# Mixing k with tokens on partitions, through the crossbar and GpSimd, with the mixes one unit ahead

## The chip, the cores and the metric

The kernel runs on one core of one Trainium2 chip. The metric is the device time of one execution in microseconds (us); lower is better. The kernel before took 245.54 us (median of 4 runs).

Engines are named as in the profile: PE is TensorE, PEld its weight loads, DVE is VectorE, ACT is ScalarE, POOL is GpSimd, and SP is the engine whose queue issues stores and crossbar transposes (DMA_TRANSPOSE in the trace: a transfer that also turns its data). A transfer lands when its data have arrived. The granted clock is the share of its full clock that PE was given. A run is called slow when it lies over 1.5% above the fastest run of the same kernel.

## The reference, cut to what matters

An attention over 4 batches of 8 heads (768 tokens, 64 columns a head, 8 blocks of 96 tokens) feeds a bilinear feed-forward layer. The argument turns on one line, the mixing of k's blocks, and on the scores that use it:

```python
k_sorted = np.einsum('bhij,bhjcd->bhicd', P, k_b).reshape(B, H, S, D)   # P: 8x8 a head, after 5 rounds
v_sorted = np.einsum('bhij,bhjcd->bhicd', P, v_b).reshape(B, H, S, D)
...
scores = scale * np.matmul(q_b, k_sb.transpose(0, 1, 2, 4, 3))          # per block of 96 tokens
...
return (a * b @ w_out)                                                   # a = x @ w_a, b = x @ w_b
```

## The kernel before

Heads are handled in 16 pairs, g = 0 to 15, four a batch. PE is kept busy with the feed-forward layer of one batch (`ffn_ab`, then `ffn_out`), and the attention of the next batch is woven in as twelve short units: `c_` mixes k and v of a pair, `s_` computes its scores, `o_` its output. A step of `ffn_ab` is eight matmuls of 384 columns.

```python
    def stage_mix(g, what, engines):                   # k and v alike
        ...
        for c in range(NCH):                           # NCH = 6
            for e in range(2):                         # the two heads of the pair
                nc.tensor.matmul(
                    mix[e * D:(e + 1) * D, c // 3, c % 3 * P:(c % 3 + 1) * P],
                    lhsT=src2[:, e, c * D:(c + 1) * D],
                    rhs=s_all[:, 2 * g + e], start=True, stop=True)
        # ... ACT (k) or DVE and ACT (v) copy mix into kT / vT, in block order
        if what == "v" and g > HP:                     # HP = 4
            nc.sync.dma_start_transpose(out=vss[...], in_=...)

    def units_full(b):
            def c_(g):
                if g < 2 * HP - 2:
                    turn_q(g)
                stage_mix(g, "k", ("act",))
                stage_mix(g, "v", ("dve", "act"))
                if 2 * HP - 2 <= g < B * HP - 2:
                    nc.gpsimd.tensor_copy(out=gate, in_=kTs[g % NBUF][0:1, 0:1])
                    load_pair((g + 2) // HP, (g + 2) % HP)     # POOL issues k, v, q
            def s_(g):
                stage_scores(g)                        # PE reads kT(g) and qT(g)
                # ... turn_v and stage_q for the first pairs, cut
                if 2 * HP <= g + 1 < B * HP:
                    pair_q(g + 1)                      # POOL copies q
                    stage_q(g + 1)                     # SP: crossbar transpose to qT
            ...
            for u, n in ((c_, 0), (s_, 0), (c_, 1), (s_, 1), (c_, 2), (o_, 0), (s_, 2), (c_, 3),
                         (o_, 1), (s_, 3), (o_, 2), (o_, 3)):
```

The gate is a copy of one element on POOL. It holds the next loads back until this unit's k has been mixed. In the timelines the matmuls of PE and the instructions of POOL and SP start in the order of the program (POOL below: gate at 102.53, then k, v and q at 103.04, 103.75 and 104.46).

The softmax here doesn't subtract the row's maximum and nothing guards it: scores larger than these inputs give would overflow.

## Time and profile before

| | before |
|---|---|
| median time, us | 245.54 |
| span of the profiled run, us | 243.3 |
| PE / DVE / ACT / POOL busy | 98% / 45% / 43% / 25% |
| granted clock of PE | 1.0 |
| time of the k and v mixes of a pair on PE, us | 0.79 |

First, from the page of the kernel before: busy us (share of the span) and the number of instructions, the busy tenths of PE in 40 slices, and the chain of work that ended last, by engine.

```profile
span 243.3 us, 5625 instructions
PE 237.4 (98%) x2309; PEld 141.6 (58%) x2309; DVE 109.1 (45%) x258; ACT 104.4 (43%) x204; POOL 61.4 (25%) x88
PE   7999999999999999999999999999999999999994
...
PE 93%; DVE 4%; ACT 1%; DMA 1%; issue 0%
```

PE is the limit from the first slice to the last. So any wait that the change puts in front of PE lengthens the run, and relief for ACT or DVE is worth nothing in itself.

Next, PE's timeline around the mixes of pair 10 (start us, duration us, engine, line, operation, output<-inputs, shape, count). The duration of a group includes the pipeline behind its last matmul, so groups are best compared from start to start.

```profile
99.90 0.81 PE L332 MATMUL pf<-xT,w_a_sb 128*128 128x384 bf16 x4
100.55 0.81 PE L332 MATMUL pf<-xT,w_b_sb 128*128 128x384 bf16 x4
101.30 0.53 PE L281 MATMUL mix<-s_all,k 128*64 128x128 bf16 x12
101.66 0.50 PE L281 MATMUL mix<-s_all,v 128*64 128x128 bf16 x12
102.09 0.82 PE L332 MATMUL pf<-xT,w_a_sb 128*128 128x384 bf16 x4
```

Four matmuls of 384 columns take 0.65 us (99.90 to 100.55), half a step. Twelve of 128 columns take only 0.36 us (101.30 to 101.66), 30 ns each. By proportion one of them alone would take about 54 ns (a third of 0.65/4 us; an estimate), so two of them run side by side in the halves of the array. In front of such a group PE pauses for 0.1 us (100.55 + 0.65 is 101.20).

Last, POOL's timeline behind the same mixes; the brackets give the idle time before and what ended it.

```profile
102.53 0.18 POOL L542 COPY gate<-kT 1x1 bf16<-1x1 bf16 x1 [4.45 <-ACT kT L162]
103.04 0.72 POOL L95 DMA_DIRECT2D k<-in_k_dram  x1 [0.34 <-PE pf L332]
103.75 0.72 POOL L95 DMA_DIRECT2D v<-in_v_dram  x1
104.46 0.73 POOL L95 DMA_DIRECT2D q<-in_q_dram  x1
105.18 0.85 POOL L246 COPY qc<-q 128x768 bf16<-128x768 bf16 x1
```

From the mix (101.30) to the end of the third load issue (105.18) POOL needs 3.9 us. Nothing that PE waits for stands behind it here, except q's copy, which has two units of time.

### The profile page before, as it was taken

How to read it: one execution, taken by the hardware profiler on the slowest of the kernel's cores; microseconds unless marked ns; L12 is line 12 of the kernel's file. 1: busy time of each engine (PE TensorE's matmuls, PEld its weight loads, DVE VectorE, ACT ScalarE, POOL GpSimd, SP SyncE). 2: the span in 40 equal slices, each digit the busy share in tenths (PEclk: the TensorE clock that was granted, in tenths of full speed). 3: DMA queues.
4: the chain of work that ended last, by engine and by line, in shares of the span. 5: the costliest groups of instructions: out<-in, count | busy, mean ns of one | idle time of the engine just before them, and what ended most of it. 6: DMA issues, size and time to landing. Idle time of an engine off the chain costs nothing.

```text
span 243.3 us, 5625 instructions
## 1 busy us (share of the span) xinstructions
PE 237.4 (98%) x2309; PEld 141.6 (58%) x2309; DVE 109.1 (45%) x258; ACT 104.4 (43%) x204; POOL 61.4 (25%) x88
## 2 busy tenths in 40 slices
PE   7999999999999999999999999999999999999994
PEld 7776666666554466666654466666654466665442
DVE  6774557555435234464534144363625144344110
ACT  3675853565630175736330165737330133333001
POOL 8766569623220053240400054200000000000000
PEclk9999999999999999999999999999999999999999
DMA  5999999985999589993964369923524310000132
GB/s 78 202 198 196 196 201 201 203 138 83 158 204 153 130 70 155 171 138 70 136 115 122 115 120 114 159 51 58 47 75 131 109 43 0 3 0 1 46 129 86
DMA packets 53930, 28.04 MB, mean 115 GB/s; under 512 B 30736, under 2 KB 50960, under 8 KB 53904
## 3 DMA queue, kind: packets, MB, share of 16 engines
q0 software_dynamic: 20944, 14.16, 41.6%
q1 hardware_dynamic: 32816, 13.45, 28.0%
q8 instruction: 18, 0.29, 0.5%
q14 instruction: 8, 0.07, 0.1%
q10 hardware_dynamic: 144, 0.07, 0.1%
HBM read 28.32 MB, written 6.29 MB: 142 GB/s over the span
## 4 chain that ended last, share of the span: by engine, by line
PE 93%; DVE 4%; ACT 1%; DMA 1%; issue 0%
PE pf L332 52%; PE po L377 24%; PE mix L281 4%; PE o_ps L231 3%; PE sc L302 2%; PE mixh L180 2%; PE po L362 1%; PE vs_ps L208 1%; PE xt_ps L222 1%; PE sc L195 1%; DMA p_nat<-in_sort_net_dram 1%; PE heat L168 1%; PE two L332 1%; PE q_ps L260 1%; DVE xp L237 1%
## 5 line engine op out<-in xcount | busy, mean ns | idle before, releaser
L353 DVE TENSOR_TENSOR hT<-a_sb,pf 128x384 bf16<-128x384 bf16 x95 | 52.6, 553 | 73.8 <-PE pf L332 46.4
L332 PE MATMUL pf<-xT,w_a_sb 128*128 128x384 bf16 x380 | 78.0, 326 | 0.2 <-ACT xT L162 0.2
L332 PE MATMUL pf<-xT,w_b_sb 128*128 128x384 bf16 x380 | 77.5, 326 | 0.0
L352 ACT CAST a_sb<-pf 128x384 bf16<-128x384 f32 x95 | 45.5, 479 | 60.9 <-PE pf L332 41.3
L377 PE MATMUL po<-w_out_sb,hT 128*128 128x512 bf16 x276 | 61.9, 379 | 0.0
L332 PEld LDWEIGHTS <-w_b_sb 128*128 128x128 bf16 x384 | 37.5, 98 | 24.8 <-issue 0.3
L332 PEld LDWEIGHTS <-w_a_sb 128*128 128x128 bf16 x384 | 34.9, 98 | 22.2
L377 PEld LDWEIGHTS <-hT 128*128 128x128 bf16 x276 | 26.3, 98 | 30.0
L162 ACT COPY o_sb<-po 128x512 f32<-128x512 f32 (+1 forms) x13 | 7.5, 577 | 46.8 <-PE po L377 45.2
L164 DVE COPY o_sb<-po 128x512 f32<-128x512 f32 (+1 forms) x12 | 7.9, 656 | 35.2 <-PE po L377 26.3
L307 ACT ACTIVATE eT<-sc 96x768 bf16<-96x768 f32 x24 | 18.0, 802 | 6.9 <-PE sc L302 6.9
L542 POOL COPY gate<-kT 1x1 bf16<-1x1 bf16 x8 | 1.4, 179 | 74.7 <-ACT kT L162 74.7
L237 DVE TENSOR_TENSOR xp<-o_ps,rec 96x512 bf16<-96x512 f32 x24 | 15.9, 684 | 0.6 <-DVE rec L235 0.2
L162 ACT CAST kT<-mix 128x384 bf16<-128x384 f32 x24 | 10.3, 482 | 8.0 <-PE mix L281 8.0
L95 POOL DMA_DIRECT2D k<-in_k_dram x16 | 11.6, 724 | 4.5 <-PE pf L332 2.3
L95 POOL DMA_DIRECT2D v<-in_v_dram x16 | 11.5, 721 | 3.1 <-DMA w_b_sb<-in_moe_w_b_dram 1.2
L231 PEld LDWEIGHTS <-eT 96*128 96x128 bf16 x256 | 10.4, 97 | 3.2 <-DVE xp L237 0.6
L235 DVE RECIPROCAL rec<-o_ps 96x8 f32<-96x8 f32 x32 | 5.6, 189 | 13.8 <-PE o_ps L231 13.8
L231 PE MATMUL o_ps<-vs,eT 96*128 96x65 bf16 x256 | 11.3, 193 | 0.2 <-DVE xp L237 0.2
L246 POOL COPY qc<-q 128x768 bf16<-128x768 bf16 x10 | 8.4, 842 | 7.2 <-DMA q<-in_q_dram 7.2
L95 POOL DMA_DIRECT2D q<-in_q_dram x12 | 8.7, 721 | 1.7 <-DMA w_a_sb<-in_moe_w_a_dram 0.7
L168 PE MATMUL heat<-warm 128*128 128x128 bf16 x84 | 7.6, 264 | 1.3 <-DVE warm L77 1.3
(80 smaller groups left out, 158.3 us busy)
## 6 DMA issues: line engine op xcount, KB each, us to landing
out_dram<-o_sb SPq DMA_DIRECT2D x17, 256.0 KB, 2.0
k<-in_k_dram POOLq DMA_DIRECT2D x16, 192.0 KB, 6.0
v<-in_v_dram POOLq DMA_DIRECT2D x16, 192.0 KB, 6.4
q<-in_q_dram POOLq DMA_DIRECT2D x12, 192.0 KB, 6.7
w_a_sb<-in_moe_w_a_dram POOLq DMA_DIRECT2D x6, 256.0 KB, 9.8
w_b_sb<-in_moe_w_b_dram POOLq DMA_DIRECT2D x6, 256.0 KB, 10.0
w_out_sb<-in_moe_w_out_dram POOLq DMA_DIRECT2D x3, 512.0 KB, 10.8
out_dram<-o_sb SPq DMA_DIRECT2D x12, 128.0 KB, 2.4
```

The lines of the kernel that those rows point to most:

```text
L95: nc.gpsimd.dma_start(out=to, in_=_ap(t, base, [[W, P], [S * D, 2], [1, W]]))
L162: nc.scalar.copy(out=out, in_=in_)
L168: nc.tensor.matmul(ps[:, 0:cols], lhsT=warm[:, 0:P], rhs=warm[:, 0:cols], start=True, stop=True)
L231: nc.tensor.matmul(o_ps[:, e, i * (D + 1):(i + 1) * (D + 1)], lhsT=eT[:, hf, e, i * BLK:i * BLK + P], rhs=vs[0:BLK, i0 + i, V0 - 1 + e * ( ...
L237: nc.vector.tensor_tensor(out=_ap(xp, i0 * 2 * D, [[nxp * 2 * D, BLK], [D, 2], [2 * D, NBH], [1, D]]), in0=_ap(o_ps, 1, [[1024, BLK], [511 ...
L246: nc.gpsimd.tensor_copy(out=qc.rearrange("p c e d -> p e c d"), in_=loaded[g][2].rearrange("p e (c d) -> p e c d", c=NCH))
L281: nc.tensor.matmul(mix[e * D:(e + 1) * D, c // 3, c % 3 * P:(c % 3 + 1) * P], lhsT=src2[:, e, c * D:(c + 1) * D], rhs=s_all[:, 2 * g + e], ...
L307: nc.scalar.activation(out=eT[:, hf, :, 0:HB], in_=sc[0:BLK, :, 0:HB], func=AF.Exp, scale=float(scale))
L332: nc.tensor.matmul(pf[:, 0:HW], lhsT=w_sb[:, kc, m * P:(m + 1) * P], rhs=x_cols(b, kc, t), start=(kc == 0), stop=(kc == KA - 1))
L352: nc.scalar.copy(out=a_sb, in_=pf[:, 0:HW])
L353: nc.vector.tensor_mul(out=hT[:, m, t * HW:(t + 1) * HW], in0=a_sb, in1=ab[1][:, 0:HW])
L377: nc.tensor.matmul(held["po"], lhsT=hTs[b][:, m, c * P:(c + 1) * P], rhs=w_out_sb[:, m, :], start=(m == 0), stop=(m == KO - 1))
```

## The change

The intent: k is mixed with tokens on partitions, which needs two matmuls of 384 columns in place of twelve of 128. The result has to be turned, so ACT copies it to `kn`, the crossbar transposes it to `kc`, and POOL puts it in block order into `kT`. To hide this longer path, the mixes run one unit ahead of the scores. This is done for pairs 5 to 15. In the diff, lines that only store a tile's name are left out.

```diff
+    def stage_k(g):
+        k2 = loaded[g][0]
+        mix = psA.tile([P, 2, 512], FP32, tag="A", name="mix")
+        for e in range(2):
+            nc.tensor.matmul(mix[:, e, 0:W], lhsT=s_all[:, 2 * g + e], rhs=k2[:, e],
+                             start=True, stop=True)
+        kn = att.tile([P, NCH, 2, D], BF16, tag="kn", name="kn", bufs=2)
+        copy("act", kn..., mix...)                       # (cut)
+        kc = att.tile([P, NCH, P], BF16, tag="kc", name="kc", bufs=3)
+        nc.sync.dma_start_transpose(out=kc, in_=kn.rearrange("p c e d -> p (c e d)"))
+    def order_k(g):
+        nc.gpsimd.tensor_copy(out=kTs[g % NBUF]..., in_=st[g, "kc"]...)   # (cut)
-            hTs[b] = ffp.tile([P, KO, S], BF16, tag="hT", name="hT")
+            hTs[b] = ffp.tile([P, KO, S], BF16, tag="hT", name="hT", bufs=1)
             def c_(g):
-                stage_mix(g, "k", ("act",))
+                if g > HP:
+                    stage_k(g)
+                else:
+                    stage_mix(g, "k", ("act",))
                 stage_mix(g, "v", ("dve", "act"))
                 if 2 * HP - 2 <= g < B * HP - 2:
-                    nc.gpsimd.tensor_copy(out=gate, in_=kTs[g % NBUF][0:1, 0:1])
+                    nc.gpsimd.tensor_copy(out=gate, in_=st[g, "kn"][0:1, 0, 0, 0:1])
                     load_pair((g + 2) // HP, (g + 2) % HP)
-            for u, n in ((c_, 0), (s_, 0), (c_, 1), (s_, 1), (c_, 2), (o_, 0), (s_, 2), (c_, 3),
-                         (o_, 1), (s_, 3), (o_, 2), (o_, 3)):
+            def run(u, g, then):
+                u(g)
+                if then is not None and g0 + then > HP:
+                    order_k(g0 + then)
+            for u, n, then in ((c_, 0, None), (c_, 1, 0), (s_, 0, None), (c_, 2, 1), (s_, 1, None),
+                               (o_, 0, None), (c_, 3, 2), (s_, 2, None), (o_, 1, 3), (s_, 3, None),
+                               (o_, 2, None), (o_, 3, None)):
```

More of the change, by code (lines that the diff above doesn't have):

```diff
@@ L293, in stage_mix @@
                                         in_=to.rearrange("p i t -> p (i t)"))
+    def stage_k(g):
[5 more added lines that the diff above has]
+        kn = att.tile([P, NCH, 2, D], BF16, tag="kn", name="kn", bufs=2)
+        copy("act", kn.rearrange("p c e d -> p e c d"),
+             mix[:, :, 0:W].rearrange("p e (c d) -> p e c d", c=NCH))
+        st[g, "kn"] = kn
+        kc = att.tile([P, NCH, P], BF16, tag="kc", name="kc", bufs=3)
+        nc.sync.dma_start_transpose(out=kc, in_=kn.rearrange("p c e d -> p (c e d)"))
+        st[g, "kc"] = kc
+    def order_k(g):
+        nc.gpsimd.tensor_copy(
+            out=kTs[g % NBUF][:, 0:S].rearrange("p (i c t) -> p c i t", i=NB, c=NCH),
+            in_=st[g, "kc"].rearrange("p c (i t) -> p c i t", i=NB))
     def stage_scores(g):
@@ L557, in o_ @@
                 to_xT(g)
-            for u, n in ((c_, 0), (s_, 0), (c_, 1), (s_, 1), (c_, 2), (o_, 0), (s_, 2), (c_, 3),
-                         (o_, 1), (s_, 3), (o_, 2), (o_, 3)):
-                us.append(lambda u=u, g=g0 + n: u(g))
+            def run(u, g, then):
[5 more added lines that the diff above has]
+                               (o_, 2, None), (o_, 3, None)):
+                us.append(lambda u=u, g=g0 + n, then=then: run(u, g, then))
             return us
```

## The prediction

> **What bounds it now.** The page shows TensorE busy 98% of 243.3 us, and the chain that ended last is 93% PE. From 40 us on PE runs from group to group almost without a gap, so each stall on PE that the change adds is paid in full, and work taken off ACT (43%), DVE (45%) or POOL (25%) is worth nothing in itself.
>
> **What the change saves on PE.** For 11 of 16 head pairs (g = 5 to 15) twelve k mixes of 128 columns (64 output rows each) become two of 384 columns. In the timeline of PE the twelve take 0.36 us from their start to the start of the v mixes (101.30 to 101.66): they run two at a time in the halves of the array. A group of four 384-column matmuls takes 0.65 us, 0.1625 us each. This agrees with the Trainium skill, page "TensorE: Matmul & The Clock Gate", section "Back-to-back issue gap" (columns/2.4 + 2.5 ns). So 0.36 becomes 0.325: 0.035 us a pair, 0.4 us in all (0.2%). The gap of 0.1 us before such a group stays with the v mixes.
>
> **What it moves.** ACT: two 0.48 us copies become one of 128x768, about 0.80 us (as eT and qT): nothing on the chain. SP: 11 more crossbar transposes, 1.2 us of issue, landing after 3 to 7 us like vs and qTf. POOL: 11 copies of 128x768, estimated at 0.84 us like qc. hT in one buffer costs nothing: PE reads the old one to the end first.
>
> **The new path to the scores.** kT is now written by POOL, in order, and the copy for pair g stands behind the next pair's unit: its gate, three load issues of 0.72 us, then the copy. Before, mix k to gate was 1.23 us (101.30 to 102.53), and the gate read only the first half; now it waits for the whole copy, +0.32. Gate to the end of the third issue took 2.65 us. So kT(g) is ready about 1.5 + 2.65 + 0.85 + 0.1 = 5.1 us after the next pair's mix starts. PE would reach the scores after 0.87 us and one to three steps of 1.30 us:
> - s(5), s(9), s(10): two steps, 3.47 us: stall about 1.7 us each
> - s(6): one step, 2.17 us: about 2.9 us
> - s(8), s(12): three steps, 4.77 us: about 0.4 us each
> - s(7), s(11), s(13) to s(15): no loads in front or enough steps: none, if the transposes land in 7 us.
>
> Sum about 8.8 us, less 0.4: +8.4 us, so 253.9; I say 253.5 us, range 248.5 to 258.0. Chances: faster 0.02, same 0.18, slower 0.80.
>
> **What would show it.** Wait list of PE: sc or its weight load of kT waiting for POOL's kT copy, 5 to 6 times, 0.3 to 3 us each, largest at the second scores of the first full batch (near 65 us); POOL's timeline: gate, k, v, q issue, kT copy. The kT copies show no idle wait for kc in those cases (if they do, the transposes are the late ones and the loss is larger). ACT's kn near 0.80 us; PE's clock stays at 1.0.
>
> **What would make it wrong.** If POOL's copy in runs of 16 is much slower than qc, or the load issues slow down beside more transposes (one showed 0.74 us extra at 88.9), the loss grows by 3 to 5 us. If crossbar transposes queue behind loads (qTf took up to 9.9 us to land), s(8), s(12), s(13) stall too. If PE's order gives more time than I count, it is a wash: 245.

## The result, and the profile after

| | before | after |
|---|---|---|
| median time, us | 245.54 | 257.77 (256.1 to 261.55, 4 runs) |
| span of the profiled run, us | 243.3 | 254.3 |
| PE busy | 98% | 94% |
| POOL busy | 25% | 28% |
| granted clock in the four runs | 1.0 in the profiled run | 0.993, 0.987, 0.980, 0.993 |

The ratio is 1.048 (95% interval 1.039 to 1.056): slower. Ratios are the mean time of one kernel's fast runs over that of the other's fast runs of the same rounds, so not quite the ratio of the medians. The run of 261.55 us is called slow.

From the page after, the same lines as before:

```profile
span 254.3 us, 5422 instructions
PE 238.6 (94%) x2188; PEld 140.5 (55%) x2199; DVE 109.2 (43%) x258; ACT 103.9 (41%) x193; POOL 70.0 (28%) x99
PE   8899999998599999699799999979999999999995
...
PE 81%; DMA 7%; POOL 3%; DVE 3%; issue 2%; ACT 2%; SPq 1%; ACTq 0%; POOLq 0%
```

PE's busy time rose by 1.2 us, though 110 weight loads and as many matmuls are gone (PEld: 2309 to 2199), and the row of tenths has holes. The list of PE's waits (us in total, times, longest) names two causes that the kernel before did not have:

```profile
PE sc L321 <- POOL kT L310: 5.3, 3, 2.6
PE sc L321 <- DMA qTf<-qc: 4.1, 2, 2.7
```

PE's timeline after, at the scores of pairs 5, 6, 9 and 10:

```profile
56.25 0.81 PE L351 MATMUL pf<-xT,w_b_sb 128*128 128x384 bf16 x4
58.39 0.52 PE L321 MATMUL sc<-qT,kT 64*128 64x96 bf16 x16 [1.32 <-POOL kT L310]
...
64.78 0.81 PE L351 MATMUL pf<-xT,w_b_sb 128*128 128x384 bf16 x4
68.18 0.51 PE L321 MATMUL sc<-qTf,kT 64*128 64x96 bf16 x16 [2.59 <-POOL kT L310]
...
105.05 0.81 PE L351 MATMUL pf<-xT,w_b_sb 128*128 128x384 bf16 x4
108.59 0.82 PE L321 MATMUL sc<-qTf,kT 64*128 64x96 bf16 x16 [2.73 <-DMA qTf<-qc]
109.34 1.46 PE L351 MATMUL pf<-xT,w_a_sb 128*128 128x384 bf16 x4
110.60 1.24 PE L351 MATMUL pf<-xT,w_b_sb 128*128 128x384 bf16 x4
111.67 0.81 PE L351 MATMUL pf<-xT,w_a_sb 128*128 128x384 bf16 x4
...
121.50 0.81 PE L351 MATMUL pf<-xT,w_b_sb 128*128 128x384 bf16 x4
123.67 0.51 PE L321 MATMUL sc<-qTf,kT 64*128 64x96 bf16 x16 [1.35 <-POOL kT L310]
```

Scores would start 0.65 + 0.10 us after the start of the group before them. Pair 5 started 1.39 us later than that (58.39 - 56.25 - 0.75), pair 6 2.65, pair 9 2.79. Behind pair 9's wait the next groups took 1.26 and 1.07 us in place of 0.65: PE ran at half its rate for a while, and with the scores themselves (0.75 us for 0.45) that cost 1.3 us more. The same reading gives 1.42 us for pair 10 (waiting for POOL's kT) and 1.45 us for pair 13 (167.38 - 165.18 - 0.75, waiting for q's transpose). Together: 1.39 + 2.65 + 2.79 + 1.33 + 1.42 + 1.45 = 11.0 us, which is the whole difference of the spans (254.3 - 243.3).

POOL's timeline after, at pair 10's unit, shows what stands in front of kT of pair 9:

```profile
103.71 0.18 POOL L564 COPY gate<-kn 1x1 bf16<-1x1 bf16 x1 [5.15 <-ACT kn L162]
104.16 0.72 POOL L95 DMA_DIRECT2D k<-in_k_dram  x1 [0.27 <-issue]
104.88 0.72 POOL L95 DMA_DIRECT2D v<-in_v_dram  x1
105.59 0.73 POOL L95 DMA_DIRECT2D q<-in_q_dram  x1
106.30 0.85 POOL L310 COPY kT<-kc 128x768 bf16<-128x768 bf16 x1
107.07 0.85 POOL L246 COPY qc<-q 128x768 bf16<-128x768 bf16 x1
```

The copy carries no idle time before it: `kc` had landed, and the copy only waited for its turn behind the three issues.

The late q has another origin. The next table puts together, for pair 9's neighbourhood, when each transfer was issued and when it landed (from the profile's records of issue and landing; "load(10)" is k, v and q of pair 10).

| | before: issued, landed | after: issued, landed |
|---|---|---|
| load(10), three transfers | 87.5 to 89.6, 94.2 to 96.3 | 91.3 to 93.5, 95.9 to 100.9 |
| load(11), three transfers | 95.1 to 96.5, 99.6 to 103.3 | 94.8 to 96.2, 103.0 to 106.4 |
| crossbar kc(9) | none | 94.3, 102.6 |
| crossbar vs(9) | 95.4, 101.6 | 95.6, 107.0 |
| crossbar qTf(9) | 91.2, 97.0 | 98.7, 108.5 |

In both kernels the six loads take about 15 us from the first issue to the last landing (87.5 to 103.3, and 91.3 to 106.4), which is 2.5 us a load as an estimate from these times. Before, the two gates lay 7.7 us apart (86.93 and 94.58), about what three loads need. After, two mixes follow each other with only two steps between, the gates lie 3.5 us apart (90.88 and 94.37), the six loads overlap, and q's transpose among them needs 9.8 us to land. That the distance of the gates does it is argued here; the later experiments limit this reading (see what stays open).

### The profile page after: what moved, and what is told of

It reads as the page before. It is cut to its first block, busy times and chain, and to the rows that moved or that the text cites. A ratio compares the mean times of both kernels' runs of the same rounds, so it can differ in the third digit from the quotient of the medians.

```text
span 254.3 us, 5422 instructions
## 1 busy us (share of the span) xinstructions
PE 238.6 (94%) x2188; PEld 140.5 (55%) x2199; DVE 109.2 (43%) x258; ACT 103.9 (41%) x193; POOL 70.0 (28%) x99
## 4 chain that ended last, share of the span: by engine, by line
PE 81%; DMA 7%; POOL 3%; DVE 3%; issue 2%; ACT 2%; SPq 1%; ACTq 0%; POOLq 0%
PE pf L351 42%; PE po L396 23%; DMA qTf<-qc 7%; PE o_ps L231 3%; PE sc L321 2%; PE heat L168 2%; PE mixh L180 2%; PE mix L281 2%; PE mix L299 1%; PE po L381 1%; POOL kT L310 1%; PE vs_ps L208 1%; POOL k L95 1%; POOL q L95 1%; PE xt_ps L222 1%
## 5 line engine op out<-in xcount | busy, mean ns | idle before, releaser
L564 POOL COPY gate<-kn 1x1 bf16<-1x1 bf16 x8 | 1.4, 178 | 72.0 <-ACT kn L162 72.0
L310 POOL COPY kT<-kc 128x768 bf16<-128x768 bf16 x11 | 9.2, 840 | 22.7 <-DMA kc<-kn 17.3
L321 PE MATMUL sc<-qTf,kT 64*128 64x96 bf16 x160 | 5.6, 211 | 8.2 <-DMA qTf<-qc 4.1
L321 PEld LDWEIGHTS <-kT 64*128 64x128 bf16 x192 | 4.8, 97 | 14.2 <-POOL kT L310 7.7
L162 ACT CAST kn<-mix 128x768 bf16<-128x768 f32 x11 | 8.8, 798 | 5.6 <-PE mix L299 5.6
```

The source lines that it names most:

```text
L162: nc.scalar.copy(out=out, in_=in_)
L310: nc.gpsimd.tensor_copy(out=kTs[g % NBUF][:, 0:S].rearrange("p (i c t) -> p c i t", i=NB, c=NCH), in_=st[g, "kc"].rearrange("p c (i t) -> ...
L321: nc.tensor.matmul(sc[:, e, i * BLK:(i + 1) * BLK], lhsT=kT[e * D:(e + 1) * D, blk * BLK:blk * BLK + P], rhs=qT[e * D:(e + 1) * D, :, blk ...
```

## The experiments

The theory: two separate harms. (1) POOL works in order, and each kT copy stands behind a gate and three load issues. (2) The order of units bunches the loads of two pairs, and the transposes land late among them. Rivals: (A) the new path of k is too long, whatever its order; (B) the crossbar cannot carry eleven more transposes; (C) the order of units alone does the harm; (D) the single buffer of hT does.

Three kernels are wrong. The comparison with the reference passed these too: with inputs of size 0.1 the scores are so small that k hardly reaches the output, so passing it says little about k. Times are medians; each call had its own runs of the kernel before on the same chip (245.11, 245.06 and 245.24 us).

### The load issues behind the copy (loads_last)

```diff
             def run(u, g, then):
                 u(g)
                 if then is not None and g0 + then > HP:
                     order_k(g0 + then)
+                if u is c_:
+                    loads(g)          # the gate and load_pair, taken out of c_
```

> The changed kernel, with the gate and the three loads of a unit put behind the kT copy on POOL. My theory: the waits of scores 5, 6 and 10 for POOL's kT copy (1.4 + 2.65 + 1.4 us in the trace of after) are gone, those of scores 9 and 13 for q's transpose stay, with the drop of the clock behind the first: about 251 us (247 to 254). Rival A, the new way of k (copy, crossbar, POOL copy) is too long whatever stands before it: 255 us or more, with PE still waiting for kT.

Measured: 252.97 us (251.77 to 255.17), ratio 1.033, inside my range. PE's timeline of this version at the scores of pairs 5 and 6:

```profile
56.33 0.81 PE L351 MATMUL pf<-xT,w_b_sb 128*128 128x384 bf16 x4
57.07 0.52 PE L321 MATMUL sc<-qT,kT 64*128 64x96 bf16 x16
...
63.46 0.81 PE L351 MATMUL pf<-xT,w_b_sb 128*128 128x384 bf16 x4
64.21 0.51 PE L321 MATMUL sc<-qTf,kT 64*128 64x96 bf16 x16
```

Both waits are gone to the last tenth (57.07 - 56.33 is 0.74), and so is pair 10's. In this batch the gates lie 8.5 us or more apart in both versions, so harm (1) stands by itself: 4.0 us at two scores came from POOL's order alone. But the median lies 2 us above what I expected, because q's wait at pair 9 grew:

```profile
PE sc L321 <- DMA qTf<-qc: 7.1, 1, 7.1
PE sc L321 <- POOL kT L310: 1.5, 1, 1.5
```

The copy of kT(8) now runs first, the second gate finds its `kn` ready, and the loads of pair 11 leave right behind it. q's transpose, issued at 96.3, landed at 110.2. But the gates lay 4.9 us apart here (88.30 and 93.20), further than the 3.5 us of the changed kernel, so closer gates don't explain why q came later. The second line is pair 7, whose `kc` landed late (69.8): 1.5 of the 4.0 us won in this batch were lost again.

### q's transpose earlier (q_early)

```diff
             def c_(g):
+                if g in (2 * HP, 3 * HP):
+                    pair_q(g + 1)
+                    stage_q(g + 1)
                 # and s_ skips these two
```

> The changed kernel, with the q of pairs 9 and 13 copied by POOL and handed to the crossbar one unit earlier, in front of the loads; the loads still stand before the kT copy. My theory: the waits for q's transpose go (2.7 + 1.4 us) and so does the drop of the clock (1.3 us); scores 5, 6, 9 and 10 still wait for POOL's kT copy by 1.4 to 2.7 us each: about 252.4 us (250 to 254), clock 1.0. If q's lateness were only hidden behind another late transfer (rival B: the crossbar is overloaded), the scores of 9 and 13 would still wait for a DMA and the time would stay at 256 or more.

Measured: 257.08 us (256.67 to 257.42), ratio 1.048, clock 0.987 in every run. A miss by 4.7 us. The waits for q did go, but pair 9 now waited 3.1 us for POOL's kT, whose `kc`, issued at 94.6, landed only at 108.1. The crowd had only been handed on: v's transpose of pair 9 took 17.0 us. The time speaks for rival B as well as for bunched loads; later experiments tell the two apart.

### Both edits (both)

> Both edits together. My theory: no stall of PE longer than 0.3 us is left in the three batches, time as before: 245.5 us (245 to 247). Rival A or B: 249 or more.

Measured: 249.32 us (246.32, 248.62, 250.02 and 255.08; the last two are slow), ratio of the fast ones 1.009. A miss: one run came near the kernel before, the others did not. The profiled run is one of the slow ones; in it pair 10 waits 3.3 us for its q, issued at 106.4 and landed at 117.4. Moving one transfer out of a crowd leaves the crowd.

### The order of units alone (order_only)

This is the kernel before, with k mixed by `stage_mix` as before, and the units in the changed order.

> The kernel before, with k mixed the old way by PE and ACT, but with the changed order of units (mixes one unit ahead). My theory: the order alone costs little, since kT needs neither crossbar nor POOL: 245 to 246.5 us. Rival C, the order itself does the harm by issuing the loads of two pairs close together, so that q's transposes of pairs 9 and 13 land late: 248 or more, with scores 9 and 13 waiting for the DMA of qTf.

Measured: 246.31 us (245.12 to 248.99), ratio 1.003 (0.9997 to 1.0059). The expectation holds for the median, and rival C falls as the cause of the whole loss. But it isn't free: three of its four runs lie above 246 us, one of them (248.99, called slow) at a clock of 0.993, and in the profiled run pair 13 waits 1.1 us for q's transpose. The trace of before has no such wait.

### The loads spread, behind the copy (spread)

The edit is shown against loads_last.

```diff
+                    by = st[g, "kn"][0:1, 0, 0, 0:1] if g % HP == 0 else \
+                        eTs[(g - (g % HP == 1)) % NBUF][0:1, 1, 0, 0:1]
+                    nc.gpsimd.tensor_copy(out=gate, in_=by)
...
-                if u is c_:
-                    loads(g)
+                if u is c_ and g % HP == 0:
+                    loads(g)
+                if u is s_:
+                    if g % HP == 0:
+                        loads(g + 1)
+                    if g % HP > 1:
+                        loads(g)
```

> The version with the loads behind the kT copy, with the loads also spread: only the first pair of a batch loads at its mix, the second waits for the first scores, the third and fourth for their own scores, so that no two pairs' loads and five crossbar transposes are in flight together. My theory (two causes: loads in front of the copy on POOL, and loads crowding the crossbar): no wait of scores above 0.5 us, transposes landing within 9 us, clock 1.0, and the time of before: 245.0 to 246.5 us. Rival A (the new way of k is too long as such): 249 or more with waits for kT at scores 5, 6 or 10. Rival B (the crossbar cannot carry eleven more transposes, however the loads lie): waits for DMA remain, 248 or more.

Measured: 245.47 us (245.21 to 246.19, 6 runs), ratio 1.0016 (1.0001 to 1.003), clock 0.999 to 1.0. The new path of k, all eleven transposes and the order of units are unchanged. What is left of the waits of scores:

```profile
PE sc L321 <- POOL kT L310: 0.5, 2, 0.3
```

The transposes of q, k and v landed within 6.0, 7.3 and 8.3 us at the latest. Rivals A and B fall: the path is short enough, and the crossbar can carry it. What mattered was where the loads stood, on POOL and in time.

### No crossbar for k (no_crossbar), and with the loads in front (no_crossbar_loads_first)

In both, POOL copies `kn` in place of `kc`, so that k's transposes are left out; the values are wrong. The first has the loads behind the copy, the second in front, as the change has them.

> WRONG VALUES ON PURPOSE: the version with the loads behind the kT copy, but POOL copies kn itself and k's crossbar transposes are left out; loads stay bunched as in the changed kernel. My theory: the late q of pair 9 (2.7 us in after, 7.1 us with the loads last) needs both the bunched loads and k's transposes: without the transposes the time is as with the order alone, 245 to 247 us, with at most about 1 us of wait for q at pair 9 or 13. Rival C (bunched loads alone make q late): 249 or more.

Measured: 250.11 us (246.9, 249.53, and 250.68 and 251.01 called slow; one of the two fast runs lies inside my range). A miss by the median and the trace: even without k's transposes, q of pair 9 landed 9.6 us after its issue and PE waited 2.0 us for it. So my sentence that the late q needs both was wrong. Bunched loads with the POOL copies between them are enough in this trace; the gates lay 4.1 us apart (87.46 and 91.52). Close gates alone are not: in order_only they lay 3.4 us apart (86.83 and 90.26), q of pair 9 landed 7.9 us after its issue, and PE did not wait for it.

> WRONG VALUES ON PURPOSE: the changed kernel, loads in front of the kT copy as it has them, but POOL copies kn itself and k's crossbar transposes are left out. My theory: the waits for POOL's copy stay as they are (scores 5: 1.4, 6: 2.7, 10: 1.4 us), because they come from POOL's order and not from the crossbar; q's wait at pair 9 becomes at most 2 us or turns into a wait of 1.4 for POOL's copy. About 252 us (249.5 to 254). Rival B (late crossbar transposes make all the waits): 247 or less.

Measured: 254.57 us (253.05 to 256.72), ratio 1.039, just above my range. PE's waits of scores in its profiled run:

```profile
PE sc L318 <- POOL kT L307: 5.3, 3, 2.6
PE sc L318 <- DMA qTf<-qc: 2.8, 1, 2.8
```

The waits for POOL are the same 5.3 us as in the changed kernel, though no crossbar feeds the copy: they come from POOL's order. Rival B's 247 or less is excluded. Only the wait of pair 13 is gone. For pair 9 my expectation missed: q still came 2.8 us late, and landed 9.9 us after its issue, against 9.8 in the changed kernel. So in this layout k's transposes are not what makes q of pair 9 late.

### The new form of the matmuls alone (form_only)

The kernel before, with the two matmuls of 384 columns and one ACT copy straight into kT; wrong values, no crossbar and no POOL copy.

> WRONG VALUES ON PURPOSE: the kernel before, in its own order, with k's twelve matmuls of 128 columns replaced by the two of 384 and one ACT copy straight into kT; no crossbar, no POOL copy. It measures what the new form is worth on PE and ACT. My theory: nothing, because the old form runs two by two and both take about 0.88 us for k and v together: 245.1 us, within 0.4 us of before. If the change's intent held (ten matmuls fewer a pair at what one of them costs when alone), 0.5 us a pair would give 240 or less.

Measured: 245.30 us (245.03 to 245.72), ratio 1.0005 (0.9992 to 1.0018). PE's timeline of this version:

```profile
93.30 0.81 PE L338 MATMUL pf<-xT,w_b_sb 128*128 128x384 bf16 x4
93.95 0.49 PE L281 MATMUL mix<-k,s_all 128*128 128x384 bf16 x2
94.37 0.53 PE L287 MATMUL mix<-s_all,v 128*64 128x128 bf16 x12
94.83 0.82 PE L338 MATMUL pf<-xT,w_a_sb 128*128 128x384 bf16 x4
```

From the end of the group before (93.95) to the next group (94.83) it is 0.88 us; before it was 0.89 (101.20 to 102.09). The pause of 0.1 us moved from in front of k to in front of v (94.37 - 93.95 is 0.42, of which 0.325 are the two matmuls). What k's two matmuls save on their twelve (0.36 to 0.325), the v mixes take back: 0.46 us from their start to the next group (94.37 to 94.83), against 0.43 before (101.66 to 102.09). The form is worth nothing here.

### One buffer for hT (ht_one)

> The kernel before with one buffer for hT, alone. My theory: no effect, 245.1 us within 0.4. Rival D (the single buffer makes the product wait at the batch's edge): 0.5 us or more a batch, 246.5 or more.

Measured: 245.23 us (244.98 to 246.05), ratio 1.0007 (0.9989 to 1.0025). Rival D falls.

### The new path without looking ahead (no_ahead)

> The version with the loads behind the kT copy, with the order of units of before: k goes through ACT, crossbar and POOL, and its scores come one to six steps of 1.3 us later. My theory: from the mix to a ready kT are 1.5 us to kn's end, 4.5 to 8 us of crossbar and 0.9 us of POOL, so scores 5 to 9, 12 and 13 each stall 3 to 5 us, about 25 us in all, and the clock drops behind the longer ones: 265 to 275 us. This is what looking ahead by one unit was for. Rival: if the new path is short enough anyway, 250 or less.

Measured, in one run (so of unknown state): 258.68 us. Slower than before by 13 us, but well short of my 265 to 275. Six scores waited for POOL's kT by 10.5 us in all, and the clock was 0.987. The size was off because I took 4.5 to 8 us for the crossbar; with the loads behind, k's transposes landed after 2.8 us in the median. So looking ahead has a use, and it was bought with the bunching.

### The changed kernel again (after_again)

> The changed kernel again, unchanged. My theory: the waits for POOL's copy at scores 5, 6 and 10 repeat to within 0.2 us in the second trace, because they come from POOL's fixed order; the waits for q and the drops of the clock behind them differ from run to run, because they come from transfers that compete: 255 to 262 us, spread of several us.

Measured: 257.31 us (253.23, 256.33, and 258.29 and 259.42 called slow), ratio 1.039. The second trace, which is of a slow run:

```profile
PE sc L321 <- POOL kT L310: 5.3, 3, 2.6
PE sc L321 <- DMA qTf<-qc: 4.2, 2, 2.8
```

The waits for POOL came at the same scores and repeated to 0.01 us (1.33, 2.60 and 1.35, against 1.32, 2.59 and 1.35). The spread of the runs goes with the clock: 253.23 us at a clock of 1.0, 256.33 at 0.993, 258.29 and 259.42 at 0.987. In this second trace a stretch at half rate also follows pair 6's wait, which the first trace doesn't show after a wait of the same length. The one run at full clock is 8.0 us above the kernel before.

## Why the prediction was right, point by point

The time on record was 253.5 us with a range of 248.5 to 258.0; 257.77 was measured, inside the range and close to its upper end. The direction was right, and so was the mechanism for the waits of pairs 5, 6 and 10, 5.5 of the 11.0 us; the sum was short by 3.8 us in the first set of medians (12.2 for 8.4). The rest, 5.6 us at pairs 9 and 13 and in the clock, came mostly from late transposes of q, which the prediction named only as a risk, and from the clock, which it held at 1.0. That the number still fell into the range is partly luck: the forecast terms of pairs 5, 6, 8, 10 and 12 were too large by 1.4 us together, which made up for part of what was missing (1.1 us at pair 9, 1.45 at pair 13, 1.3 of the clock).

- **POOL's order.** "kT is now written by POOL, in order, and the copy for pair g stands behind the next pair's unit." Shown by the timeline after, by loads_last (the waits of pairs 5, 6 and 10 vanish) and by no_crossbar_loads_first (they stay without the crossbar). Predicted and measured: pair 5, 1.7 and 1.39 us; pair 6, 2.9 and 2.65; pair 10, 1.7 and 1.42. Each was about 0.3 us too large.
- **Pairs 8 and 12.** Predicted 0.4 us each; 0.1 each was measured.
- **Pair 9, the mis-sized term.** Predicted 1.7 us for POOL's copy; 2.79 us was measured, and the last thing to come was q's transpose. The prediction held this open only under what would make it wrong ("if crossbar transposes queue behind loads"), and there it named pairs 8, 12 and 13. POOL's copy for pair 9 ended only at 107.15 (106.30 + 0.85), so about 1.4 of the 2.79 us would have been waited for it in any case (an estimate from this trace, 107.15 + 0.05 - 105.80). I took the landing times of before over to an order of units in which two pairs' loads leave 3.5 us apart in place of 7.7.
- **Pair 13, a missing term.** "None, if the transposes land in 7 us" became 1.45 us, since q's transpose took 8.2 us to land.
- **"PE's clock stays at 1.0".** Wrong. The profiled run lost 1.3 us behind pair 9's wait, and two of the other three runs had a lower clock still (0.987 and 0.980 for its 0.993). The run at full clock (253.23 us) lies where the prediction stood; it left no trace, so whether its waits are the predicted ones is not shown.
- **The gain on PE.** Predicted 0.4 us, or 0.035 a pair; the timeline gives 0.01 a pair, and form_only no gain that could be told from zero. The pause stayed in front of the v mixes, as predicted, but these took 0.03 us longer, and with that the saving was gone.
- **The small parts.** ACT's copy took 0.798 us (0.80 predicted), POOL's copy 0.84 us in the median (0.84), hT's single buffer cost nothing.

On the Trainium skill: "TensorE: Matmul & The Clock Gate", section "Part 3: Packing small matmuls — row/col tiling", says that matmuls in different tiles of the array run concurrently, and the 30 ns a matmul of the old form agree: this is why removing ten of twelve instructions saved nothing. "DMA: Bandwidth & Descriptors", section "SWDGE vs HWDGE vs iDMA", says that transfers issued by GpSimd and those issued by SP feed different queues inside the same engines, which take turns; the landing times here fit that, but no run here shows the turns themselves.

What stays open: the shares of the crossbar and of the bunching in pair 9's wait. Bunched loads can make it without k's transposes (no_crossbar), spread loads with the crossbar don't (spread). One trace each says what k's transposes add: with the loads in front of the copy nothing (q landed after 9.8 us with them, 9.9 without), with the loads behind it 4.3 us (13.9 in loads_last, 9.6 in no_crossbar). And the distance of the gates doesn't fix the landing by itself: at 3.4 us PE did not wait for pair 9 (order_only), at 4.9 it waited 7.1 us (loads_last). What decides it is not shown. Nor was the loads' place in front of the copy tried with spread loads; only the first of the three batches of this path, where the loads were not bunched, stands for it. No version beat the kernel before: the best, spread, is at 1.0016.

## What to carry to other kernels

Before work is moved to an engine with free time, look at what stands in front of it in that engine's order: POOL was idle for three quarters of the run, and yet a copy of 0.84 us came 1.4 to 2.7 us late, because three load issues stood before it. When units are reordered, the loads tied to them are reordered as well: check how far apart they leave and which transfers will be under way with them, and don't carry a transfer's landing time over from the old order. And on a PE that is 98% busy, count array time from start to start and not instructions: twelve matmuls that run two by two cost no more than two large ones.

## What the Trainium skill lacked or had wrong

- "TensorE: Matmul & The Clock Gate", "Why this matters for your kernels", asks for no gaps over about 3 us. Here half rate followed waits of 2.73 us (after) and even 2.0 us (no_crossbar: groups of 0.65 us took 1.28), while after waits of 2.60 and 2.59 us it came in one trace (after_again) and not in the other (after). In these traces a gap of 2.0 us was not always safe, which is less than the page says; no half rate followed the waits of 1.9 us and less.
- The same page, "Back-to-back issue gap", gives 131 ns a matmul for 512 columns in a real stream. Here six matmuls of 512 columns took 1.29 us from start to start (71.73 to 73.12 in after, less the pause of 0.1), 215 ns each; the page's formula for a matmul by itself fits, its figure for the stream doesn't. No page gives a time for the pause in front of a group that works in halves of the array: 0.1 us here.
- "GPSIMD Engine Reference" gives no time that an ordinary load issue holds POOL's order: 0.72 us each here, with 0.27 to 0.34 us between the gate and the first.
- "DMA: Bandwidth & Descriptors", "DMA Transpose (X-bar)", gives no landing time beside loads: 2.8 us when alone, 9.8 us among six loads (q, after), 17.0 us at worst (v, q_early).
